# Retention with a gated MLP on one core: in the late second products, the last columns' load and scaling four steps behind the stretch, and the third stretch at step 21 in place of 20

## The chip, the cores and the metric

The kernel runs on one core of a Trainium2 chip. It is written engine by engine: PE (TensorE) multiplies matrices, and its weight loads are shown as PEld; DVE (VectorE), ACT (ScalarE) and POOL (GpSimd) work on tiles; SP (SyncE) issues nearly all of the DMAs. Each engine runs its own list of instructions in a fixed order. The metric is the device time of one execution in microseconds (us).

## What is computed

The reference, cut to what matters:

```python
scores = matmul(q, k^T) / 8                      # 8 batches, 8 heads, 576 positions, 64 wide
ret    = scores * Dmat                           # Dmat[i, j] = gamma_h ** (i - j) for i >= j, else 0
attn   = matmul(ret, v)                          # -> x: 4608 tokens x 512
h      = x @ w_in                                # 512 -> 2048
g      = h - tanh(h)
out    = g @ w_out                               # 2048 -> 512
```

## The kernel before

**Tiling.** The 576 positions of each batch are cut into 9 chunks of 64. A *column block* n is one chunk position of all 8 batches, 512 tokens. Retention goes chunk by chunk: the scores within a chunk, plus a running `state` per batch and head that carries what lies before. Each product is made in three parts, of a high and a low word of the operands (`xh`/`xl` with two words of `w_in`; `gh`/`gl` with two words of `w_out`), so a first product `mm1(n, f)` (L385) is 12 matmuls of 128x128 by 512, and a second product `mm2(n, f)` (L451) is 12 as well, three for each of the four output banks `o0` to `o3`.

**Stages.** At first the weights come in and are split into words; in that time the first products of column blocks 0 and 1 are made, and most of them are written to a spill buffer in DRAM. Then comes the *late* loop, which this case is about: 32 steps, `late = [(1, f) ...16..., (0, f) ...16...]`, each of them one second product of column block 1 (steps 0 to 15), then of block 0 (steps 16 to 31). After it, column blocks 2 to 8 run with first and second products in turn.

**A step k of the late loop** puts on the engines, in this order:
- `words(k+1)`: ACT makes the high word `gh` of the fetched column (L433), DVE the low word `gl` (L434);
- `resume(k+2)`: ACT takes the tanh `th` (L426), DVE subtracts it (L427);
- `fetch(k+4)`: SP issues the DMA of the column `s` from the spill buffer (L421). It goes into one of 3 buffers, so it waits for the `gl` of the column three before it;
- `mm2(k)`: PE makes the product. At step 15, the last one of block 1, the four banks finish one after another, and `store` copies them out: ACT `o0` and `o2` (L468), DVE `o1` and `o3` (L470); SP then issues 8 DMAs to the output (L472). Step 16 starts to fill the same four banks.

In the prediction, "the column of step 17" is the one that mm2 of step 17 uses. It is fetched at step 13, and its tanh stands on ACT in step 15, just ahead of the copies of `o0` and `o2`.

**Stretches.** Ahead of steps 3, 13 and 20 stands `entry3`, a *stretch* of retention matmuls (64x64, L257) for block 2 and the next pair's scores: batches 0 and 1 at step 3, 2 to 4 at step 13, 5 to 7 at step 20. Its end loads the data of what comes next on SP and scales it on POOL (`prep`, L207): `vr` (v and k rows, 512 KB), where it is wanted `one` (a single batch, 512 KB), and `qk` (q and k columns, 512 KB). `qk` is scaled by a table `qtab` of its column block. `qtab` has one buffer; when the pair to load is the first of a new block, `load_part` loads that block's table first (L162), and this DMA waits until POOL has made its last scaling by the old table. At step 13 the pair to load is the first of block 3, so that is where the table changes.

**Order.** `in_order` (last line of `retention_ffn`) ties every instruction to the one before it on its engine, so each engine's list, SP's too, is as the code is written. A DMA that waits on SP holds up all the DMAs behind it.

Of the kernel before, what the change touches and what calls it, by code (L numbers as in the profile page):

```python
# [59 lines left out]
def behind(tc, name):  # L60

    tc.add_manual_dep(
        tc.nc.cur_bb.bb.instructions[-1], name,
        mybir.DependencyInfo(mybir.DependencyClass.Sync, mybir.DependencyReason.DATA), reason="paced",
    )
# [3 lines left out]
def retention_ffn(ctx: ExitStack, tc: tile.TileContext, ins, out, spill):  # L69
# [86 lines left out]
    def load_qtab(c):  # L156
        if c not in qtabs:
            if c == 1:
                qtabs[c] = const.tile([P, 4, C], F32, tag="wo6", name="qtab1")
            else:  # L160
                qtabs[c] = pool.tile([P, 4, C], F32, tag="qtab", bufs=1, name=f"qtab{c}")
            nc.sync.dma_start(qtabs[c], qtab_d[c - 1])  # L162

    def load_part(j, t):

        if j >= NI:
            return
        c, b = divmod(j, B)
        if t == 0:
            load_qtab(c)  # L170
        early = c == 1 and b // 2
        if early and early > 1:

            part = const.tile([P, 2, 2, 4, C], F32, tag=f"wo{2 * (early - 2) + t}", name=f"early{j}_{t}")
        elif early and t == 1:
            part = pool.tile([P, 2, 2, 4, C], F32, tag="one", bufs=1, name=f"vr{j}")
        else:
            part = pool.tile([P, 2, 2, 4, C], F32, tag=("qk", "vr")[t], bufs=2 - t, name=f"{('qk', 'vr')[t]}{j}")
        nc.sync.dma_start(part, qkv_d[c - 1, b : b + 2, :, 2 * t : 2 * t + 2].rearrange("u p t i s -> p u t i s"))
        if early and early > 1:  # L180
            behind(tc, pace[-1])
        parts[j, t] = part
        for u in range(2):
            loaded.setdefault(j + u, Parts([None, None])).parts[t] = part[:, u]
# [12 lines left out]
    def prep(j, t, n=2):  # L197

        if j >= NI:
            return  # L200
        c = j // B
        a = parts[j, t][:, :, 0]
        if t == 0:
            table = qtabs[c].unsqueeze(1).broadcast_to([P, n, 4, C])
        else:
            table = vtab[:, c].unsqueeze(1).unsqueeze(3).broadcast_to([P, n, 4, D])
        nc.gpsimd.tensor_tensor(a, a, table, op=ALU.mult)  # L207
# [16 lines left out]
    def m_score(j, sc):  # L224
        a = loaded[j]
        return [
            (sc[half(c), i], a[half(c), 1, i, :], a[half(c), 0, i, :], True, True) for i in range(4) for c in range(2)
        ]

    def m_state(j, new):  # L230
        a = loaded[j]
        return [
            (
                new[half(c), i],
                krows[j // 4][half(c), j % 4, i, :] if j < B else a[half(c), 3, i, :],
                a[half(c), 2, i, :], True, True,
            )
            for i in range(4) for c in range(2)
        ]
# [12 lines left out]
    def run(same, other):  # L252

        while same or other:
            for ms in (same, other):
                for out_, w, x, start, stop in ms[:2]:
                    nc.tensor.matmul(out_, w, x, start=start, stop=stop)  # L257
                del ms[:2]

    def after_score(j, sc, n):  # L260

        if j < B:

            pm = pool.tile([P, 2, 4, C], F32, tag="gh", name=f"pm{j}")
            nc.vector.tensor_tensor(pm[:, 0], sc[:, 0], decay, op=ALU.mult)
        else:

            pm = parts[j, 0][:, :, 1]
            nc.vector.tensor_tensor(
                pm, sc, mask.unsqueeze(1).unsqueeze(1).broadcast_to([P, n, 4, C]), op=ALU.mult,  # L270
            )
        for u in range(n):
            scored[j + u] = pm[:, u]
# [20 lines left out]
    def bank(name, tag):  # L294
        return psp.tile([P, 2, 4, D], F32, tag=tag, bufs=2 if tag == "h" else 1, name=name)
# [5 lines left out]
    def pair(what, j, bank):  # L301
        return what(j, bank[:, 0]) + what(j + 1, bank[:, 1])
# [10 lines left out]
            more[1]()  # L313
        add_state(j, new)

    def entry3(j):


        c0, b = divmod(j, B)
        single, states = b > 0, c0 < NC - 1  # L320
        then = j + 2 + single
        o = bank(f"own{j}", "own")
        outs, scores = pair(m_out, j, o), []
        if single:
            two = bank(f"two{j + 2}", "new")
            run(m_score(j + 2, two[:, 1]), outs[:8])
            after_score(j + 2, two[:, 1:], 1)
            outs = outs[8:]
            if states:

                new = bank(f"new{j + 2}", "h")
                run(m_state(j + 2, new[:, 0]), outs[:8])
                outs = outs[8:]
                kept = pool.tile([P, 1, 4, D], F32, tag="cv", bufs=4, name=f"kept{j + 2}")
                nc.scalar.copy(kept, new[:, :1])
        if states:
            new = bank(f"new{j}", "h")
            run(pair(m_state, j, new), outs[:16])
            outs = outs[16:]
        if single:  # L340
            if not states:
                run([], outs)
            outs = m_out(j + 2, two[:, 0], True)
            if states:
                add_state(j, new)
            low = after_out(j, o, 2, False)
        if then < NI:
            sc = bank(f"s{then}", "h")
            scores = pair(m_score, then, sc)
        run(scores, outs)  # L350
        if not single:
            if states:
                add_state(j, new)
            low = after_out(j, o, 2, False)
        low()
        if then < NI:
            after_score(then, sc, 2)
        if single:
            if states:
                add_state(j + 2, kept, 1)  # L360
            after_out(j + 2, two[:, :1], 1)

        more = then % B > 0
        if then < NI:
            load_part(then, 1)
            prep(then, 1)
            if more:
                load_one(then + 2)
                prep(then + 2, 1, 1)
                prep(then + 2, 0, 1)  # L370
            load_part(then + 2 + more, 0)
            prep(then + 2 + more, 0)


    gs, ops, homes, obs = {}, {}, {}, {}
# [211 lines left out]
    first = 2 * B  # L587
    for k, (n, f) in enumerate(seq):
        last_two = k - (len(seq) - 2)
        if k in (2, 7):  # L590
            scale_k(k // 4)
        if k + 1 in early:
            scale_v(2 * early[k + 1])
        if last_two < 0:
            step()
        else:
            fetch(*late[2 + last_two])
        mm1(n, f, ("h", "o2", "h", "o3")[k % 4] if k < len(seq) - 4 else ("o2", "o3", "h", "h")[k % 4])
        if last_two < 0:
            step()  # L600
            if k < 24:
                step()
        if k in scales:
            scale_q(2 * scales[k])
        upto("load", k + (7 if k < 11 else 6))
        if k in (2, 5):
            load_pair(B + 4 + 2 * (k - 2) // 3)
        if k in (9, 10):
            load_part(first, k - 9)
        for f in [f for f in home if home[f] == (7, 13, 12, 11, 10)[k - NF]] if NF <= k < NF + 5 else []:  # L610
            nc.sync.dma_start(spill[0, f], homes[home[f]][:, (f + 1) % 2 if f > 1 else f])
        if k == 3:
            nc.sync.dma_start(krows[1], krows_d[1])
            behind(tc, pace[-1])
            sc = scores_of(3)
            ms, done = first_states(0, "new")
            run(pair(m_score, B, sc) + ms, [])
            after_score(B, sc, 2)
            done()
        if k in early:  # L620
            p = early[k]
            more = first_states(2 * (p - 3), f"o{(p + 1) % 2}") if p < B - 1 else None
            entry(2 * p, scores_of(p), more)
        if k == 14:
            load_part(first + 2, 0)
        if k == 26:
            prep(first, 1)
        if k == 28:
            prep(first + 2, 0)
    for k, (n, f) in enumerate(late):  # L630
        if k in (3, 13, 20):
            entry3(first + (0, 2, 5)[(3, 13, 20).index(k)])
        if 0 < k < len(late) - 1:
            words(*late[k + 1])
        if k < len(late) - 2:
            resume(*late[k + 2])
        if k + 4 < len(late):
            fetch(*late[k + 4])
        for _ in range(2 if k < 4 else 1):
            step()  # L640
        if k < len(late) - 1:
            mm2(n, f)
# [70 lines left out]
```

## Time and profile before

| what | value |
|---|---|
| time, median of 3 runs | 894.35 us (893.67 to 894.58) |
| time of the profiled execution | 894.74 us |
| its span, first to last instruction | 893.0 us |
| DVE busy | 368.8 us (41%) |
| ACT busy | 293.5 us (33%) |
| POOL busy | 70.3 us (8%) |
| DMA moved | 82.06 MB, mean 92 GB/s |
| late loop on PE | about 122 to 225 us of the span |

Times in the views are microseconds from the start of the span. A row of the timeline gives start, duration, engine, line, operation, output<-inputs, shapes, count, and in brackets how long the engine was idle before it and what ended that. A row of the waits gives who waited for whom, the total, the number of times and the longest. A row of the windows gives a stretch of time and the busy time of each engine in it, the TensorE clock that was granted (1.00 is full), the busy share of the DMA engines and GB/s. A row of the chain gives start, duration and what the chain ran through. Matmuls are pipelined: a 128x512 one is listed with 0.39 us while the next one starts 0.23 us later.

### The profile page before, as it was taken

The numbers are of one execution on the slowest core, as the hardware profiler recorded it, in microseconds if no ns is written. First come the engines' busy times: TensorE is split into PE (matmuls) and PEld (weight loads), VectorE is DVE, ScalarE is ACT, GpSimd is POOL, SyncE is SP. The second block draws the span as 40 slices with busy tenths as digits, with TensorE's granted clock in tenths as the row PEclk, the third lists the DMA queues.
The fourth block names the chain that finished last, engine by engine and source line by source line (L and its number), as shares of the span: only waits on it lengthen the run. The fifth ranks groups of instructions, "written<-read, shape, count | busy, mean of one in ns | idle before, by whom it ended". The sixth has DMA issues, their size and how long they took to land.

```text
span 893.0 us, 17735 instructions
## 1 busy us (share of the span) xinstructions
PE 874.8 (98%) x7848; PEld 723.6 (81%) x7848; DVE 368.8 (41%) x568; ACT 293.5 (33%) x522; POOL 70.3 (8%) x73
## 2 busy tenths in 40 slices
PE   7999999799999999999999999999999999999998
PEld 6777887588888888888888888888888888888886
DVE  6889876455333233323332334233332423223222
ACT  4787764334222222222222222222222322222222
POOL 0001002200011011101110101101110111000000
PEclk9999999999999999999999999999999999999999
DMA  9966955452212032202320131103220321002001
GB/s 346 360 201 217 345 169 166 136 160 78 60 61 77 1 95 72 79 1 64 103 69 10 49 111 44 43 6 90 72 78 1 93 73 49 1 1 47 1 1 47
DMA packets 37725, 82.06 MB, mean 92 GB/s; under 512 B 4241, under 2 KB 5393, under 8 KB 37649
## 3 DMA queue, kind: packets, MB, share of 16 engines
q1 hardware_dynamic: 37120, 80.02, 28.2%
q8 instruction: 61, 1.00, 0.5%
q10 hardware_dynamic: 528, 0.92, 0.3%
q14 instruction: 16, 0.12, 0.0%
HBM read 63.62 MB, written 17.30 MB: 91 GB/s over the span
## 4 chain that ended last, share of the span: by engine, by line
PE 85%; DMA 5%; DVE 4%; ACT 3%; issue 1%; POOL 0%; SPq 0%; DVEq 0%; POOLq 0%; ACTq 0%
PE o L451 42%; PE h L385 36%; DMA rwo<-in_w_out_dram 2%; PE new L257 2%; PE s L257 2%; PE own L257 1%; PE two L257 1%; DMA rwi<-in_w_in_dram 1%; DMA s<-spill_dram 1%; DVE mo L111 0%; DMA vr<-in_qkv_dram 0%; DVE mo L113 0%; DVE s L427 0%; DVE mo L106 0%; DMA spill_dram<-g 0%
## 5 line engine op out<-in xcount | busy, mean ns | idle before, releaser
L385 PE MATMUL h<-xh,wi 128*128 128x512 f32 x1152 | 302.4, 390 | 2.9 <-issue 1.1
L451 PE MATMUL o<-wo,gh 128*128 128x512 f32 x1144 | 292.3, 394 | 6.3 <-ACT ob L468 6.0
L451 PEld LDWEIGHTS o<-wo,gh 128*128 128x128 f32 x1144 | 213.9, 189 | 53.1 <-ACT ob L468 6.5
L385 PEld LDWEIGHTS h<-xh,wi 128*128 128x128 f32 x1152 | 215.3, 188 | 49.6 <-ACT wi L118 1.6
L412 DVE TENSOR_TENSOR g<-h,g 128x512 f32<-128x512 f32 x114 | 78.8, 691 | 341.4 <-ACT g L411 341.3
L411 ACT ACTIVATE g<-h 128x512 f32<-128x512 f32 x114 | 68.2, 598 | 364.2 <-PE h L385 362.5
L451 PE MATMUL o<-wo,gl 128*128 128x512 f32 x572 | 157.6, 390 | 0.0
L385 PE MATMUL h<-xl,wi 128*128 128x512 f32 x576 | 154.1, 389 | 0.0
L385 PEld LDWEIGHTS h<-xl,wi 128*128 128x128 f32 x576 | 108.1, 188 | 22.7
L451 PEld LDWEIGHTS o<-wo,gl 128*128 128x128 f32 x572 | 107.7, 188 | 22.6
L414 DVE TENSOR_TENSOR gl<-g,gh 128x512 fp32r<-128x512 f32 x113 | 81.4, 720 | 77.6 <-ACT gh L413 75.5
L413 ACT CAST gh<-g 128x512 fp32r<-128x512 f32 x113 | 70.1, 621 | 85.7 <-DVE g L412 85.7
L207 POOL TENSOR_TENSOR vr<-vr,vtab 128x512 f32<-128x512 f32 x21 | 23.1, 1100 | 626.9 <-DMA vr<-in_qkv_dram 540.9
L257 PE MATMUL own<-qk,state 64*64 64x64 f32 x736 | 45.2, 221 | 0.0
L257 PE MATMUL own<-qk,vr 64*64 64x64 f32 x736 | 44.1, 218 | 0.0
L257 PEld LDWEIGHTS own<-qk,vr 64*64 64x64 f32 x736 | 36.8, 135 | 0.0
L257 PEld LDWEIGHTS own<-qk,state 64*64 64x64 f32 x736 | 36.7, 134 | 0.0
L434 DVE TENSOR_TENSOR gl<-s,gh 128x512 fp32r<-128x512 f32 x30 | 22.7, 757 | 25.4 <-PE o L451 13.5
L207 POOL TENSOR_TENSOR qk<-qk,qtab 128x512 f32<-128x512 f32 x20 | 27.7, 1385 | 46.7 <-DMA qk<-in_qkv_dram 46.7
L433 ACT CAST gh<-s 128x512 fp32r<-128x512 f32 x30 | 18.6, 621 | 33.2 <-PE o L451 20.3
L427 DVE TENSOR_TENSOR s<-s,th 128x512 f32<-128x512 f32 x30 | 22.7, 757 | 8.1 <-ACT th L426 8.1
L257 PE MATMUL s<-qk 64*64 64x64 f32 x736 | 25.5, 219 | 0.0
(82 smaller groups left out, 560.6 us busy)
## 6 DMA issues: line engine op xcount, KB each, us to landing
qk<-in_qkv_dram SPq DMA_DIRECT2D x23, 512.0 KB, 5.8
vr<-in_qkv_dram SPq DMA_DIRECT2D x23, 512.0 KB, 4.4
out_dram<-ob SPq DMA_DIRECT2D x69, 128.0 KB, 2.4
rwi<-in_w_in_dram SPq DMA_DIRECT2D x16, 512.0 KB, 5.7
rwo<-in_w_out_dram SPq DMA_DIRECT2D x16, 512.0 KB, 5.3
s<-spill_dram SPq DMA_DIRECT2D x30, 256.0 KB, 2.7
one<-in_qkv_dram SPq DMA_DIRECT2D x14, 512.0 KB, 5.1
spill_dram<-g SPq DMA_DIRECT2D x20, 256.0 KB, 4.5
```

The lines of the kernel that those rows point to most:

```text
L207: nc.gpsimd.tensor_tensor(a, a, table, op=ALU.mult)
L257: nc.tensor.matmul(out_, w, x, start=start, stop=stop)
L385: nc.tensor.matmul(hp, win[f][:, a, cc, :], x[:, cc, :], start=(k == 0), stop=(k == 3 * NCC - 1))
L411: nc.scalar.activation(g, h, AF.Tanh)
L412: nc.vector.tensor_tensor(g, h, g, op=ALU.subtract)
L413: nc.scalar.copy(gh, g)
L414: nc.vector.tensor_tensor(gl, g, gh.bitcast(F32), op=ALU.subtract)
L427: nc.vector.tensor_tensor(g, g, th, op=ALU.subtract)
L433: nc.scalar.copy(gh, g)
L434: nc.vector.tensor_tensor(gl, g, gh.bitcast(F32), op=ALU.subtract)
L451: nc.tensor.matmul(ops[n][t], g[:, t * P : (t + 1) * P], wout[f_][:, a, :], start=(f_ == first and k == 0), stop=(f_ == final and k == 2),)
```

## The change

`entry3` is given a list; if it is there, the load of the last `qk` (with its table, where that is due) and its scaling are not issued at the stretch's end, but noted. The late loop issues them four steps later: for the stretch of step 3 at step 7, for that of step 13 at step 17. The third stretch stands at step 21 in place of 20, and its last load at step 25. The loads of `vr` and `one` stay at the stretches. The stretches of the later column blocks are called as before.

```diff
-    def entry3(j):
+    def entry3(j, later=None):
...
-            load_part(then + 2 + more, 0)
-            prep(then + 2 + more, 0)
+            if later is None:
+                load_part(then + 2 + more, 0)
+                prep(then + 2 + more, 0)
+            else:
+
+                later.append(then + 2 + more)
...
+    rest = []
     for k, (n, f) in enumerate(late):
-        if k in (3, 13, 20):
-            entry3(first + (0, 2, 5)[(3, 13, 20).index(k)])
+        if k in (3, 13, 21):
+            entry3(first + (0, 2, 5)[(3, 13, 21).index(k)], rest)
+        if k - 4 in (3, 13, 21):
+            load_part(rest[0], 0)
+            prep(rest.pop(), 0)
```

**SP around the second stretch.** SP's list from the stretch of step 13 to step 17, before (`s_1` is the column of step 17, `s_4` that of step 20, `ob` the output of block 1, `qtab` and `qk` the table and first pair of block 3):

```order
L193 DMA one_2087<-in_qkv_dram 128x1024
L162 DMA qtab_2091<-in_qtab_dram 128x256
L179 DMA qk_2093<-in_qkv_dram 128x2x512
L421 DMA s_1_2103<-spill_dram 128x512
L421 DMA s_2_2124<-spill_dram 128x512
L421 DMA s_3_2145<-spill_dram 128x512
L472 DMA out_dram<-ob_2150 64x512 x8
L421 DMA s_4_2179<-spill_dram 128x512
L421 DMA s_5_2204<-spill_dram 128x512
```

And the same place in the changed kernel:

```order
L193 DMA one_2087<-in_qkv_dram 128x1024
L425 DMA s_1_2098<-spill_dram 128x512
L425 DMA s_2_2119<-spill_dram 128x512
L425 DMA s_3_2140<-spill_dram 128x512
L476 DMA out_dram<-ob_2145 64x512 x8
L425 DMA s_4_2174<-spill_dram 128x512
L162 DMA qtab_2192<-in_qtab_dram 128x256
L179 DMA qk_2194<-in_qkv_dram 128x2x512
L425 DMA s_5_2204<-spill_dram 128x512
```

The table and the pair have moved past four fetches and the eight stores. In the same way the `qk` of the first stretch moves from ahead of the fetch of step 7's column to behind that of step 10's.

**DVE around the third stretch.** DVE's list there, before (`gl_5`, `s_5` belong to the column of step 21, `s_6` to that of step 22; `one<-two,mask` masks the single batch's scores within the stretch):

```order
L427 TENSOR_TENSOR s_5_2204<-s_5_2204,th_5_2243 128x512
L269 TENSOR_TENSOR one_2087<-two_2261,mask 128x256
L299 TENSOR_TENSOR state<-new_2298,state 128x512
L286 TENSOR_TENSOR xl_1748<-own_2260,xh_1747 128x2x4x64
L269 TENSOR_TENSOR qk_2093<-s_2333,mask 128x2x256
L299 TENSOR_TENSOR state<-kept_2296,state 128x256
L285 TENSOR_TENSOR xl_1748<-two_2261,xh_1747 128x4x64
L434 TENSOR_TENSOR gl_5_2378<-s_5_2204,gh_5_2377 128x512
```

And in the changed kernel:

```order
L431 TENSOR_TENSOR s_5_2204<-s_5_2204,th_5_2243 128x512
L438 TENSOR_TENSOR gl_5_2261<-s_5_2204,gh_5_2260 128x512
L431 TENSOR_TENSOR s_6_2225<-s_6_2225,th_6_2264 128x512
L269 TENSOR_TENSOR one_2087<-two_2282,mask 128x256
L299 TENSOR_TENSOR state<-new_2319,state 128x512
L286 TENSOR_TENSOR xl_1748<-own_2281,xh_1747 128x2x4x64
L269 TENSOR_TENSOR qk_2194<-s_2354,mask 128x2x256
```

The stretch's DVE work stands one step later: `gl_5` and the subtraction for `s_6` now come ahead of the mask. On ACT the stretch's copies move past `gh_5` and `th_6` in the same way, and on PE its matmuls past the 12 of step 20.

## The prediction

> **What bounds the kernel now.** The page's first row says that PE is busy for 98% of the span:
>
> ```profile
> PE 874.8 (98%) x7848; PEld 723.6 (81%) x7848; DVE 368.8 (41%) x568; ACT 293.5 (33%) x522; POOL 70.3 (8%) x73
> ```
>
> The change removes no matmul, so it can only gain what PE waits. That is the second view, the waits of PE, longest first:
>
> ```profile
> PE o L451 <- ACT ob L468: 6.0, 1, 6.0
> ...
> PE o L451 <- ACT gh L433: 0.2, 1, 0.2
> ```
>
> One wait is larger than all others together, and both rows lie in the late loop. The timeline of PE shows where:
>
> ```profile
> 171.65 0.39 PE L451 MATMUL o<-wo,gl 128*128 128x512 f32 x1
> 178.08 4.21 PE L451 MATMUL o<-wo,gh 128*128 128x512 f32 x8 [6.04 <-ACT ob L468]
> ```
>
> Step 15 ends at 171.65; step 16 wants its first bank at 171.88 (a matmul every 0.23 us) and gets it at 178.08. It waits for ACT's copy of `o0`, so ACT's timeline is next:
>
> ```profile
> 169.56 0.62 ACT L433 CAST gh<-s 128x512 fp32r<-128x512 f32 x1 [1.73 <-DVE s L427]
> 176.92 0.63 ACT L426 ACTIVATE th<-s 128x512 f32<-128x512 f32 x1 [6.75 <-DMA s<-spill_dram]
> 177.46 1.05 ACT L468 COPY ob<-o 128x512 f32<-128x512 f32 x2
> ```
>
> The two copies stand behind the tanh of step 17's column, and that waited for its DMA. Why that came late is seen on SP, first its longest wait between 160 and 186, then its timeline:
>
> ```profile
> SPq L162 <- POOL one L207: 6.1, 1, 6.1
> ```
>
> ```profile
> 163.79 0.71 SPq L193 DMA_DIRECT2D one<-in_qkv_dram  x1
> 170.66 0.33 SPq L162 DMA_DIRECT2D qtab<-in_qtab_dram  x1
> 171.04 0.43 SPq L179 DMA_DIRECT2D qk<-in_qkv_dram  x1
> 171.56 1.36 SPq L421 DMA_DIRECT2D s<-spill_dram  x3
> 178.05 6.25 SPq L472 DMA_DIRECT2D out_dram<-ob  x8
> ```
>
> POOL's rows close the chain:
>
> ```profile
> 167.35 1.57 POOL L207 TENSOR_TENSOR vr<-vr,vtab 128x512 f32<-128x512 f32 x1 [24.61 <-DMA vr<-in_qkv_dram]
> 168.88 1.06 POOL L207 TENSOR_TENSOR one<-one,vtab 128x256 f32<-128x256 f32 x1
> 169.90 0.73 POOL L207 TENSOR_TENSOR one<-one,qtab 128x256 f32<-128x256 f32 x1
> 176.38 1.27 POOL L207 TENSOR_TENSOR qk<-qk,qtab 128x512 f32<-128x512 f32 x1 [5.75 <-DMA qk<-in_qkv_dram]
> ```
>
> SP could not overwrite `qtab` before POOL's last scaling by it ended at 170.63; then 512 KB of `qk` went ahead of the fetch, which reached ACT at 176.92. So: table, SP, fetch, tanh, copy, bank, PE.
>
> The stall has a tail. The windows show the granted clock (the third last column), the chain of waits the pace:
>
> ```profile
> 172.00:175.80 3.80, 0.04 (x1) 0.00 (x0) 0.00 (x0) 0.00 (x0) 0.00 (x0) 1.00 0.93 266
> 175.90:178.00 2.10, 0.00 (x0) 0.00 (x0) 0.42 (x1) 1.08 (x3) 1.27 (x1) 0.50 0.41 156
> 178.10:182.60 4.50, 4.44 (x10) 3.16 (x11) 2.57 (x5) 1.74 (x4) 0.00 (x0) 0.50 0.51 118
> ```
>
> ```profile
> 178.93 12.70 PE o L451 x47
> ...
> 194.59 30.15 PE o L451 x132
> ```
>
> The clock halves near 175.85, 3.8 us after PE's last matmul, and is full again near 182.65. At full clock a matmul takes 30.15/132 = 0.228 us.
>
> **The change part by part.** All times are those of the profile before.
>
> *A, the stall.* 178.08 - 171.88 = **6.2 us**. How early the fetch for step 17 can now be there follows from the page's median for such a fetch and from DVE's row that frees its buffer:
>
> ```profile
> s<-spill_dram SPq DMA_DIRECT2D x30, 256.0 KB, 2.7
> ```
>
> ```profile
> 165.31 0.68 DVE L434 TENSOR_TENSOR gl<-s,gh 128x512 fp32r<-128x512 f32 x1
> ```
>
> In the changed order it stands right behind `one` and waits only for its buffer, free at 165.98. It lands between 2.7 us later, 168.7, and 5.3 later (171.56 to 176.92, behind `qk`), 171.3. I take 169.2: `one` was there by 168.88. All 6.2 us go, and what is late next is D.
>
> *B, the half clock.* The 48 matmuls from 178.08 to 178.93 + 12.70 = 191.63 take 13.5 us; at 0.228 they take 10.9. **2.5 us** go (0.1 off for the change to the stretch). They go only if no new wait of some 3.8 us comes. A short one is cheap: behind 1.08 us of idle time PE runs six matmuls in 1.55 us, full pace:
>
> ```profile
> 42.79 1.55 PE L385 MATMUL h<-xh,wi 128*128 128x512 f32 x6 [1.08 <-issue]
> ```
>
> The Trainium skill, "TensorE: Matmul & The Clock Gate", Part 1, says that the clock halves after an idle window of about 3.4 us and comes back after about 3.4 us of work. The windows agree in kind, but show 4.6 us to come back; an estimate by the page is 3.4/2 = 1.7 us for B, and the sum below would be 0.8 smaller, 887.0.
>
> *C, step 7.* The same pattern, small:
>
> ```profile
> 142.74 1.07 PE L451 MATMUL o<-wo,gl 128*128 128x512 f32 x4
> 144.06 1.20 PE L451 MATMUL o<-wo,gh 128*128 128x512 f32 x4 [0.25 <-ACT gh L433]
> ```
>
> ```profile
> 141.46 0.63 ACT L426 ACTIVATE th<-s 128x512 f32<-128x512 f32 x1 [0.88 <-DMA s<-spill_dram]
> ```
>
> Due at 142.74 + 4 x 0.228 = 143.65, come at 144.06: **0.4 us**. Its fetch came 0.88 late to ACT behind the first `qk`, which now goes behind step 10's fetch.
>
> ```profile
> 151.66 0.62 ACT L433 CAST gh<-s 128x512 fp32r<-128x512 f32 x1 [1.02 <-PE o L451]
> ```
>
> That `qk` goes out some 10 us later and is wanted at 162.5 (the row of `two` in E). It now holds up step 11's fetch by about 1 us, whose `gh` has room: it waits for PE, not for the fetch, and stands 2.7 us ahead of step 11 (144.06 + 4 x 2.73 = 155.0). Nothing.
>
> A + B + C = **9.1 us**. Against it stand three new waits.
>
> *D, the handover at step 16.* With the fetch in time, ACT does `gh` to 170.18, tanh 170.1 to 170.7, `o0` to 171.2, `o2` to 172.0 (PE ends that bank at 171.4). DVE:
>
> ```profile
> 167.94 1.53 DVE L427 TENSOR_TENSOR s<-s,th 128x512 f32<-128x512 f32 x1
> 170.21 0.98 DVE L434 TENSOR_TENSOR gl<-s,gh 128x512 fp32r<-128x512 f32 x1 [0.74 <-ACT gh L433]
> ...
> 178.19 1.28 DVE L470 COPY ob<-o 128x512 f32<-128x512 f32 x2
> ```
>
> `gl` to 171.2, the subtraction to 171.8, `o1` to 172.4, `o3` to 173.0. PE wants `o1` at 172.1 and has it at 172.45, `o3` at 172.9 and has it at 173.0: **0.45 us**. Least: 0. Most, with the fetch landing at 171.3: `o0` ready at 172.45, `o1` at 173.35, `o3` at 173.95: 0.6 + 0.65 + 0.15 = 1.4.
>
> *E, the third stretch.* Where a stretch wants its scaled pair and its mask is read from the one of step 13:
>
> ```profile
> 160.62 0.27 PE L257 MATMUL two<-one 64*64 64x64 f32 x2
> 162.55 0.23 PE L257 MATMUL two<-one 64*64 64x64 f32 x2
> ```
>
> ```profile
> 161.35 0.42 DVE L269 TENSOR_TENSOR one<-two,mask 128x256 f32<-128x256 f32 x1 [1.98 <-PE two L257]
> ```
>
> Both are wanted 1.93 us behind its start, where the scores of the next pair and the masked product (the second row of `two`) begin; the mask itself takes 0.42. Step 16 starts at 171.88, so the stretch of step 21 stands 0.45 (D) + 5 x 2.72 later, at 185.9, and wants both at 187.85.
>
> Table and `qk` now go out behind the stores. Stores from 171.6, 6.25 us as before, to 177.85; fetch for step 20 at 177.9, table 178.4, `qk` 178.8. `qk` reaches POOL 5.3 us on as before (171.04 to 176.38), at 184.1, and is scaled at 185.4: 2.4 us of margin, where at step 20 it would be 0.3 short. But the fetch for step 21 goes behind `qk` and lands near 184.7 (as 176.92 to 171.04). Tanh, subtraction, `gh` end at 186.8, step 22's tanh at 187.3, and on DVE `gl`, step 22's subtraction and only then the stretch's mask at 188.4: **0.5 us** of wait. Least 0 (stores 0.5 us quicker do it). Most 1.35: step 21's subtraction falls beside POOL's scaling of `qk`, and D's first row took 1.53 us beside POOL where A's `gl` took 0.68 without, 0.85 more.
>
> Here a rule speaks against the change, since `qk`'s scaling lay in the stall so far, where DVE had little to do. The Trainium skill, "SBUF — State Buffer", "SBUF: two separate sides", says that POOL and a DVE operation with both inputs in SBUF share ports by an exclusive lock: whoever is first holds it to its end. D's row agrees. By the rule step 21's subtraction waits up to the rest of a 1.27 us scaling, an estimate of 0.8 us more, and the sum is 887.0.
>
> *F, step 20.* Its fetch goes out at 177.9 behind the stores, lands 2.7 later at 180.6; tanh, subtraction and `gh` (0.6 to 0.7 us each with gaps between, 2.1) end at 182.7. Step 20 starts at 183.2: **0**, with 0.5 us to spare. Most, landing after 5.3: 185.3, a wait of 2.1.
>
> Moving the third stretch by one step moves its matmuls past 12 others: nothing in itself. Its `vr` and `qk` go out 5 to 10 us later and are wanted at the next stretch, which comes after the late loop: nothing.
>
> Sum: 9.1 - 0.45 - 0.5 = **8.15 us** off. The profiled execution takes 894.74 (span 893.0 and 1.74 around it): 886.6. The median of the three runs is 0.39 lower, so I forecast **886.2 us**.
>
> **The rivals.**
> *New waits in steps 16 to 21* (0.22). The load that blocked SP is not gone; it stands behind eight stores, in front of step 21's fetch. With D and F at their worst 3.5 of the 9.1 come back: 894.35 - 5.6 = **888.7**. For it: F's margin is only 0.5 us and SP's stores took 6.25 us. Against: each wait moves the later ones' due times back, so they don't add up.
> *The change doesn't free the copies* (0.05). If the fetch for step 17 is slow because the DMA engines are full (0.93 busy from 172.0 to 175.8) and not because it was issued late, ACT waits as before: **894.3**. Against: from 163.9 on only `vr` and `one` are ahead of it, and both were there by 168.9.
> *Slower* (0.03). `qk` misses the third stretch. It loses as much as was won when the scaled pair comes 6.2 us after its due time 187.85 (6.2 of waiting and 2.5 of half clock), at 194 in place of 185.4. Two more us make it **896.3**. That needs the stores to hold SP for 15 us in place of 6.25; the longest wait of SP in this stretch is 6.1.
>
> **How the numbers follow.** The forecast, with D to F between 0 and some 2 us, has 0.70: 885.2 to 887.3. The rivals have 0.22, 0.05 and 0.03. The range starts at 9.1 off less 0.3 of scatter (the three runs lie 0.9 apart), 884.9, and ends at 889.3, above the first rival. A measurement of this kernel tells 0.2%, 1.8 us, from no change: faster 0.92 (forecast and first rival), same 0.05, slower 0.03.
>
> **What would show it.** In the changed profile: no wait of PE for ACT's copies over 1 us; granted clock 1.00 from 172 to 190; the fetch for step 17 out at about 165.6 and its tanh right behind the `gh` before it; no wait at step 7; SP's 6.1 us wait for POOL gone at the second stretch; the third stretch within a microsecond of 185.5. Wrong would be: a PE wait at step 20 or in the stretch of step 21 on ACT, DVE or POOL's `qk`, or the old wait with its 6 us.

## The result and the profile after

| kernel | time, median | ratio to before, 95% interval |
|---|---|---|
| before | 894.47 us (893.67 to 895.04, 4 runs) | |
| changed | 887.30 us (887.15 to 889.93, 3 runs, and one run of 3106.18, not counted) | 0.993 [0.9906, 0.9953] |
| changed again (e1) | 886.78 us (886.58 to 887.28, 5 runs) | 0.9906 [0.9886, 0.9926] |
| changed, third time (e9) | 886.94 us (885.64 to 889.54, 6 runs) | 0.9914 [0.9898, 0.993] |

The change makes the kernel faster by 0.7 to 0.9%, and no interval holds 1. One run of the changed kernel, the one first profiled, took 3106 us with every kind of matmul slowed throughout and DVE and ACT at their usual pace; nothing is read from it, and "after" below is e1, the same kernel profiled again.

The waits of PE in the late loop of e1, to set against the 6.0 and the 0.2 us of before:

```profile
PE two L257 <- DVE one L269: 0.5, 1, 0.5
PE o L455 <- DVE ob L474: 0.2, 1, 0.2
```

The two old waits are gone and two small new ones have come, at other places. (This view counts idle time of PE alone; what each place lost in all stands in the table below.) The granted clock (third last column) stays full where it was halved:

```profile
165.00:172.00 7.00, 6.83 (x31) 5.36 (x30) 5.51 (x8) 3.95 (x8) 3.21 (x3) 1.00 0.60 175
172.00:176.00 4.00, 4.00 (x17) 3.08 (x18) 2.67 (x5) 1.62 (x3) 0.00 (x0) 1.00 0.60 178
176.00:190.00 14.00, 13.41 (x236) 11.02 (x236) 5.96 (x11) 4.59 (x9) 1.29 (x1) 1.00 0.64 181
```

SP's timeline in e1 shows why: behind `one` stands no table and no wait for POOL, but the fetches.

```profile
163.22 0.86 SPq L193 DMA_DIRECT2D one<-in_qkv_dram  x1
165.44 5.52 SPq L425 DMA_DIRECT2D s<-spill_dram  x3
171.05 6.55 SPq L476 DMA_DIRECT2D out_dram<-ob  x8
177.69 0.54 SPq L425 DMA_DIRECT2D s<-spill_dram  x1
178.31 0.40 SPq L162 DMA_DIRECT2D qtab<-in_qtab_dram  x1
178.77 0.42 SPq L179 DMA_DIRECT2D qk<-in_qkv_dram  x1
179.28 0.89 SPq L425 DMA_DIRECT2D s<-spill_dram  x2
```

The fetch for step 17 goes out at 165.44, where it went at 171.56, and ACT shows no wait for it:

```profile
169.51 0.63 ACT L430 ACTIVATE th<-s 128x512 f32<-128x512 f32 x1
170.04 0.57 ACT L472 COPY ob<-o 128x512 f32<-128x512 f32 x1
```

**A finer measure.** The runs of one kernel lie up to 5.5 us apart (before, 17 runs beside e1: 892.66 to 898.16), and in the profiles the late loop starts anywhere between 121.8 and 123.8 us, before the change can act. So I also use the **late loop**: PE's time from the first matmul of step 0 to the first first product of block 2. Before and e1, PE's timeline, first and last row of it:

```profile
122.23 1.98 PE L451 MATMUL o<-wo,gh 128*128 128x512 f32 x8
...
224.58 0.39 PE L385 MATMUL h<-xh,wi 128*128 128x512 f32 x1
```

```profile
122.32 1.98 PE L455 MATMUL o<-wo,gh 128*128 128x512 f32 x8
...
217.16 0.39 PE L389 MATMUL h<-xh,wi 128*128 128x512 f32 x1
```

That is 102.35 us before and 94.84 after, **7.5 us** less. A step's 12 matmuls take 2.72 us where nothing is late. What a step took above that (a step's own spacing from its first matmul to the next step's or stretch's first; a step ahead of a stretch is set against 2.81 us and the third stretch against 2.96, which they take where nothing is late), by PE's rows:

| place | before | e1 | forecast for e1 |
|---|---|---|---|
| steps 6 and 7 (term C) | 0.57 | 0.03 | 0 |
| wait at step 16 (A) | 6.20 | 0 | 0 |
| half clock in step 16 (B) | 2.48 | 0 | 0 |
| handover in step 16 (D) | in A | 0.64 | 0.45 |
| wait in the third stretch (E) | 0 | 1.13 | 0.5 |
| step 20 (F) | 0 | 0.05 | 0 |

### The profile page after: what moved, and what is told of

Read it like the earlier page. It is cut to its first block, busy times and chain, and to the rows that moved or that the text cites. A ratio compares the mean times of both kernels' runs of the same rounds, so it can differ in the third digit from the quotient of the medians.

```text
span 3104.4 us, 17735 instructions
## 1 busy us (share of the span) xinstructions
PE 3098.4 (100%) x7848; PEld 1715.7 (55%) x7848; DVE 367.1 (12%) x568; ACT 295.0 (10%) x522; POOL 66.9 (2%) x73
## 4 chain that ended last, share of the span: by engine, by line
PE 100%; ACT 0%; DVE 0%; issue 0%
PE o L455 46%; PE h L389 46%; PE new L257 3%; PE s L257 2%; PE own L257 1%; PE two L257 1%; PE new_first L257 0%; PE wps L502 0%; PE s_first L257 0%; PE own_first L257 0%; DVE ob L489 0%; ACT ob L488 0%; ACT xh L283 0%; DVE warm L496 0%
## 5 line engine op out<-in xcount | busy, mean ns | idle before, releaser
L389 PE MATMUL h<-xh,wi 128*128 128x512 f32 x1152 | 1014.5, 1091 | 0.5 <-ACT xh L283 0.5
L455 PE MATMUL o<-wo,gh 128*128 128x512 f32 x1144 | 985.4, 1096 | 0.0
L389 PEld LDWEIGHTS h<-xh,wi 128*128 128x128 f32 x1152 | 507.9, 441 | 436.6 <-issue 433.7
L455 PEld LDWEIGHTS o<-wo,gh 128*128 128x128 f32 x1144 | 485.8, 426 | 434.6 <-issue 427.7
L389 PE MATMUL h<-xl,wi 128*128 128x512 f32 x576 | 514.9, 1099 | 0.0
L455 PE MATMUL o<-wo,gl 128*128 128x512 f32 x572 | 514.6, 1088 | 0.0
L389 PEld LDWEIGHTS h<-xl,wi 128*128 128x128 f32 x576 | 239.0, 415 | 230.9 <-issue 230.9
L455 PEld LDWEIGHTS o<-wo,gl 128*128 128x128 f32 x572 | 231.5, 405 | 230.1 <-issue 229.8
L257 PE MATMUL own<-qk,vr 64*64 64x64 f32 x736 | 123.3, 447 | 0.0
L257 PEld LDWEIGHTS s<-qk 64*64 64x64 f32 x736 | 77.9, 367 | 5.8 <-issue 5.8
```

Of the source, the lines that this page charges most:

```text
L389: nc.tensor.matmul(hp, win[f][:, a, cc, :], x[:, cc, :], start=(k == 0), stop=(k == 3 * NCC - 1))
L455: nc.tensor.matmul(ops[n][t], g[:, t * P : (t + 1) * P], wout[f_][:, a, :], start=(f_ == first and k == 0), stop=(f_ == final and k == 2),)
```

## The experiments

Each kernel was profiled once and timed beside the kernel before, in three groups: e1 to e4, e5 to e8, and e9 to e11. Medians can be compared within a group, ratios across groups. The short diffs are against the changed kernel.

| kernel | late loop, us | time, median, us | ratio to before, 95% interval |
|---|---|---|---|
| before | 102.35 | 895.37, 893.85, 895.10 beside the three groups | |
| e2 stretch at 21 alone | 102.09 | 895.74 | 1.0005 [0.9991, 1.0019] |
| e1, e9 changed | 94.84, 94.71 | 886.78, 886.94 | 0.9906 and 0.9914, above |
| e3 late loads alone | 94.93 | 888.13 | 0.9919 [0.9901, 0.9938] |
| e4 first load at once | 95.67 | 887.42 | 0.9912 [0.9893, 0.9931] |
| e7 only the table late | 94.92 | 887.58 | 0.9932 [0.9919, 0.9944] |
| e6 copies ahead of the tanh | 93.60 | 885.96 | 0.9915 [0.9902, 0.9929] |
| e5, e10 load behind the fetch | 93.58, 93.76 | 886.26, 886.62 | 0.9913 [0.99, 0.9927], 0.9905 [0.9891, 0.9919] |
| e8 both | 93.67 | 886.1 | 0.992 [0.9907, 0.9933] |
| e11 load behind the fetch, stretch at 20 | 94.92 | 886.91 | 0.9915 [0.99, 0.9929] |

The intervals of the times tell e2 from all others, and little else; what follows on parts of a microsecond rests on the late loop of one profile each (two for the changed kernel and for e5).

**e1: the changed kernel again.**

> The changed kernel once more, since its first profile shows every matmul of the program slowed. Theory (chain of table, SP, fetch, tanh, copy, bank): A, B and C are gone, and what is left is D at step 16 (0.45 us) and E in the stretch of step 21 (0.5 us): span 884.8, time 886 to 887.5, granted clock 1.00 through 172 to 190. Rival (new waits in steps 16 to 21): a wait of 1 to 3 us at step 20 or in the stretch of step 21, time 888 to 890.

By the time, the clock (1.00) and the span (885.5 where 884.8 was expected) this is the theory's side. But the two new waits add up to 1.8 us in place of 0.95, and the larger one, 1.13 us in the stretch of step 21, is as long as the rival said (1 to 3 us). What sets them is read in the points below.

**e2: the third stretch at step 21, all loads at once.**

```diff
-            entry3(first + (0, 2, 5)[(3, 13, 21).index(k)], rest)
-        if k - 4 in (3, 13, 21):
-            load_part(rest[0], 0)
-            prep(rest.pop(), 0)
+            entry3(first + (0, 2, 5)[(3, 13, 21).index(k)])
```

> The third stretch at step 21, all loads at the stretches as before. Theory: the 6.2 us stall at step 16, the half clock and the 0.4 us at step 7 are all there, and the move itself is worth nothing: 894.0 to 894.8, as before the change. Rival (the place of the third stretch is what helps): below 892.

The waits of PE in its late loop, and a window of it:

```profile
PE o L455 <- ACT ob L472: 5.6, 1, 5.6
PE o L455 <- ACT gh L437: 0.6, 1, 0.6
```

```profile
175.10:181.80 6.70, 4.06 (x9) 2.88 (x10) 3.09 (x5) 2.64 (x5) 1.26 (x1) 0.50 0.63 184
```

Both waits and the half clock are there, with 5.6 and 0.6 us where they were 6.0 and 0.2. The median lies above the expected 894.8, as does that of the kernel before beside it, 895.37. The move alone is worth nothing; the gain belongs to the late loads.

**e3: the late loads alone**, `(3, 13, 20)` in both lines.

> The late loads with the third stretch still at step 20. Theory: A, B and C are gone as in e1; the pair for the third stretch is scaled at about 185.4 where step 20 wants it at 185.1, and its mask stands behind the subtraction for step 21, whose fetch went behind qk: 0.3 to 1.5 us of wait in the stretch in place of e1's 0.5, time 0 to 1.5 us above e1. Rival (the move to step 21 costs as much as it saves): the same as e1 within 0.3 us.

Late loop 94.93 against 94.84 and 94.71: in the stretch e3 loses as much as e1 does (1.17 and 1.13 us). PE stops at two places, and the second stop is for the mask:

```profile
184.87 0.33 PE L257 MATMUL s<-qk 64*64 64x64 f32 x4 [0.20 <-issue]
185.62 0.27 PE L257 MATMUL two<-one 64*64 64x64 f32 x2 [0.42 <-DVE one L269]
```

The first stop looks like the pair, but POOL ended the pair's scaling at 184.58, 0.3 us ahead of the row. What ended 0.1 us ahead of it is a copy on ACT, which empties the bank that the new scores take:

```profile
184.41 0.35 ACT L335 COPY kept<-new 128x256 f32<-128x256 f32 x1
```

This copy stands behind the tanh of the column whose fetch went behind `qk`, as the mask does on DVE. So in e3 as in e1 the late fetch sets the wait, with the pair only 0.1 us behind the 184.5 at which the stretch wanted it. By the late loop the rival holds: with the other edit as it is, the move to step 21 neither gains nor costs. The times don't decide it: the medians lie 1.3 us apart, which the theory allows, but e3's six runs spread over 3 us, 886.5 to 889.52, and the profiled one is the second fastest of them.

**e4: the first stretch's load at once**, `rest if k > 3 else None`.

> As the changed kernel, but the first stretch loads its qk at once, as before; only the second and third loads are late. Theory: the wait at step 7 is back, 0.4 us above e1, all else as e1. Rival (the 0.4 us are absorbed by a later wait): the same as e1.

```profile
PE o L455 <- ACT gh L437: 0.9, 1, 0.9
PE two L257 <- DVE one L269: 0.3, 1, 0.3
PE o L455 <- DVE ob L474: 0.2, 1, 0.2
```

The wait at step 7 is back, larger than before the change (0.9 against 0.2 in the view of the waits; 0.6 in e2). Steps 6 and 7 lose 1.2 us, three times what C says. ACT's tanh shows the cause, a fetch for which ACT sat idle 2.57 us; DVE's subtraction behind it took its usual 0.69 us:

```profile
143.10 0.63 ACT L430 ACTIVATE th<-s 128x512 f32<-128x512 f32 x1 [2.57 <-DMA s<-spill_dram]
```

The late loop is only 0.8 us longer than e1's, since the wait in the stretch is 0.61 in place of 1.13. That is no answer to the lateness of PE at step 7, which moves the copies and the stores just as far; what sets that wait is seen under e9.

**e7: only the table and the scaling late.**

```diff
-    def load_part(j, t):
+    def load_part(j, t, table=True):
...
-        if t == 0:
+        if t == 0 and table:
             load_qtab(c)
...
+                load_part(then + 2 + more, 0, False)
                 later.append(then + 2 + more)
...
-            load_part(rest[0], 0)
+            load_qtab(rest[0] // B)
             prep(rest.pop(), 0)
```

> As the changed kernel, but only the table and the scaling are four steps late; the 512 KB of qk go out at the stretch as before the change, ahead of the fetches. Theory (the stall was SP held by the table): SP isn't held, qk lands near 170.3 and the fetch for step 17 near 171, so step 16 waits 1.0 to 1.6 us in place of 0.64 with the clock at 1.00, the wait at step 7 is back (0.5), and the stretch of step 21 waits 0 to 0.2: late loop 94.6 to 95.6. Rival (512 KB ahead of the fetch are what hurts): step 16 waits 3 us or more, late loop above 97, with the half clock above 99.

PE's waits at step 16 and ACT's tanh ahead of the copies, e7's timeline:

```profile
171.87 0.50 PE L456 MATMUL o<-wo,gh 128*128 128x512 f32 x1 [0.46 <-ACT ob L473]
172.72 0.50 PE L456 MATMUL o<-wo,gh 128*128 128x512 f32 x1 [0.35 <-DVE ob L475]
```

```profile
170.71 0.63 ACT L431 ACTIVATE th<-s 128x512 f32<-128x512 f32 x1 [1.73 <-DMA s<-spill_dram]
```

With 512 KB of `qk` ahead of it and SP free, the fetch was there at 170.7: steps 15 and 16 lose 1.5 us (0.6 and 0.9) where e1 loses 0.64, and the granted clock stays at 1.00 from 165 to 183. So of the old stall, SP held by the table made nearly all; the 512 KB ahead make 0.9 us of it. This is also the test of the rival that the fetch was slow because the DMA engines were full: from its issue at 165.38 to the tanh at 170.71 it took 5.3 us, as long as before the change (171.56 to 176.92), so it had been late because it was issued late. In the stretch of step 21 PE loses nothing: there the fetch for step 21 stands behind the table alone.

**e5 and e10: the late load behind its step's fetch.**

```diff
-        if k - 4 in (3, 13, 21):
-            load_part(rest[0], 0)
-            prep(rest.pop(), 0)
...
         if k + 4 < len(late):
             fetch(*late[k + 4])
+        if k - 4 in (3, 13, 21):
+            load_part(rest[0], 0)
+            prep(rest.pop(), 0)
```

> As the changed kernel, but the late load stands behind its step's fetch on SP, not ahead of it: the fetch for step 21 no longer follows qk. By late loop I mean PE's time from the first matmul of step 0 to the first first product of block 2; it was 94.84 us in e1, with 1.13 us of wait in the stretch of step 21. Theory (that wait is the fetch for step 21, late behind qk, and through it the mask): the fetch lands near 182 in place of 184.9, qk is scaled 0.4 us later at about 186.1 and wanted at 187.6, the stretch waits 0 to 0.2 us, late loop 93.6 to 93.9. Rival (the wait is POOL's scaling of qk or DVE beside it): still 0.8 us or more, late loop 94.5 or more.

> e5 once more, beside e9. Theory: late loop 93.5 to 93.7, no wait in the stretch of step 21, 0.6 to 1.3 us below e9. Rival (e5's gain was another chip's scatter): within 0.3 us of e9's late loop.

DVE's timeline up to the mask, first e1, then e5:

```profile
185.61 0.69 DVE L431 TENSOR_TENSOR s<-s,th 128x512 f32<-128x512 f32 x1 [2.17 <-ACT th L430]
187.04 0.69 DVE L438 TENSOR_TENSOR gl<-s,gh 128x512 fp32r<-128x512 f32 x1 [0.74 <-ACT gh L437]
187.65 0.68 DVE L431 TENSOR_TENSOR s<-s,th 128x512 f32<-128x512 f32 x1
188.25 0.42 DVE L269 TENSOR_TENSOR one<-two,mask 128x256 f32<-128x256 f32 x1
```

```profile
184.03 1.09 DVE L438 TENSOR_TENSOR gl<-s,gh 128x512 fp32r<-128x512 f32 x1 [0.74 <-ACT gh L437]
185.04 0.68 DVE L431 TENSOR_TENSOR s<-s,th 128x512 f32<-128x512 f32 x1
185.94 0.42 DVE L269 TENSOR_TENSOR one<-two,mask 128x256 f32<-128x256 f32 x1 [0.22 <-PE two L257]
```

In e1 the mask comes behind a row of column work that started late; in e5 that work is done and the mask waits for PE. The stretch loses nothing, in both profiles; the late loop is 1.0 to 1.3 us below the changed kernel's. The chain fetch, tanh, subtraction, mask is confirmed. (One figure of the theory was off: the pair was scaled at 184.57 in e5, not at 186.1, though its load went out behind the fetch.) In the time itself e10 lies 0.3 us below e9, less than the runs scatter.

**e6: at step 15 the product and the copies ahead of the tanh.**

```diff
-        if k < len(late) - 2:
+        if k < len(late) - 2 and k != 15:
             resume(*late[k + 2])
...
             mm2(n, f)
+        if k == 15:
+            resume(*late[k + 2])
```

> As the changed kernel, but at step 15 the product and the copies of the banks stand ahead of the tanh and subtraction for step 17. Theory: the wait at step 16 (0.64 us in e1) goes, since DVE copies o1 one subtraction earlier, but the third stretch is then wanted 0.6 us earlier while its late fetch is set by SP's stores, so its wait grows from 1.13 to about 1.7: late loop 94.6 to 94.9, no gain. Rival (the two waits are independent): late loop 94.2.

Neither side: 93.60 is below both. Step 16 still takes 0.43 us too long, since bank 3 is only done when step 15 ends and its copy takes 0.7; and the stretch waits 0.20, not more than in e1. The stores went out earlier against PE: 0.74 us ahead of step 16's first matmul, 0.26 in e1, and took 6.0 us in place of 6.5. How much of that is the edit and how much the chance of a run was not tried apart.

**e8: e5 and e6 together.**

> e5 and e6 together: the late load behind its step's fetch, and at step 15 the copies ahead of the tanh. Theory: both new waits go, late loop 93.0 to 93.4, about 1.6 us below e1. Rival (the stretch then comes so early that qk, scaled at about 186, is late for it): wait of 0.5 us or more on POOL's qk at step 21, late loop 93.7 or more.

Late loop 93.67, no wait in the stretch, 0.4 us at step 16 in place of 0.6, and 0.3 us lost in steps 5 and 6, ahead of all that was edited (what costs them is read under C below). Above the expected 93.0 to 93.4 and no better than e5 or e6 alone.

**e9: the changed kernel a third time.**

> The changed kernel once more, beside e10 and e11 on one chip. Theory: late loop 94.3 to 94.9; the wait in the stretch of step 21 (1.13 us in e1, 0.61 in e4) goes with how long SP takes to issue the eight stores (6.5 us in e1, 5.9 in e4), the wait at step 16 is 0.6 again. Rival (the wait in the stretch is fixed by DVE's order): 1.1 again whatever the stores take.

Late loop 94.71, step 16 loses 0.62. The stores and the loss in the stretch, from SP's and PE's rows: e1 6.55 and 1.13 us, e9 5.81 and 0.72, e4 5.91 and 0.61. SP in e9:

```profile
171.91 5.81 SPq L476 DMA_DIRECT2D out_dram<-ob  x8
```

Longer stores go with a longer wait from e1 to the other two, but between e9 and e4 the order is turned round: the stores are not all of it. The size follows from when the fetch for step 21 arrives, that is, when its tanh starts on ACT. First e1, then e9:

```profile
184.94 0.63 ACT L430 ACTIVATE th<-s 128x512 f32<-128x512 f32 x1 [2.23 <-DMA s<-spill_dram]
185.29 0.63 ACT L430 ACTIVATE th<-s 128x512 f32<-128x512 f32 x1 [2.60 <-DMA s<-spill_dram]
```

| kernel | tanh for step 21 | stretch starts | tanh ahead by | stretch loses |
|---|---|---|---|---|
| e1 | 184.94 | 185.71 | 0.77 | 1.13 |
| e9 | 185.29 | 186.48 | 1.19 | 0.72 |
| e4 | 186.05 | 187.34 | 1.29 | 0.61 |
| e6 | 185.23 | 186.93 | 1.70 | 0.20 |

The last two columns add up to 1.90 or 1.91 us each time, and in e5, where the tanh is 3.27 us ahead, nothing is lost. So the arrival of this fetch alone gives the size of the wait; the stores act through it, and so does the fetch's own way behind `qk`.

**e11: e5 with the third stretch at step 20.**

> e5 with the third stretch back at step 20. In e5 the pair was scaled 13.8 us behind the start of step 16; at step 20 the stretch wants it 13.5 us behind. Theory: with the fetch out of the way the pair itself is the last to come, the stretch waits 0.3 to 1.2 us for POOL's qk, late loop 93.9 to 94.8; that is what the move to step 21 is worth. Rival (the place of the stretch doesn't matter, as e3 against e1): within 0.2 us of e10.

Late loop 94.92, 1.2 us above e10 (in the time 0.3 us, less than the scatter) and 0.1 above what was expected. PE and POOL in e11:

```profile
187.12 0.27 PE L257 MATMUL s<-qk 64*64 64x64 f32 x2 [0.83 <-POOL qk L207]
```

```profile
185.79 1.27 POOL L207 TENSOR_TENSOR qk<-qk,qtab 128x512 f32<-128x512 f32 x1 [14.45 <-DMA qk<-in_qkv_dram]
```

Here the stretch waits for the pair alone, and step 21 is the place where it doesn't. The size is that of one profile: the pair was scaled 14.5 us behind the start of step 16, where e5 and e10 had it 13.8 behind, which would have left some 0.3 us of wait. The move has a use, but only once the fetch is out of the way (e3 against e1: 0.1 to 0.2 us; e11 against e10: 1.2 us).

## Why the prediction was right, point by point

The forecast was 886.2 us with 884.9 to 889.3; three measurements gave 887.3 (by the ratio, 0.993 x 894.47 = 888.2), 886.8 and 886.9. The runs of one kernel lie up to 5.5 us apart, so a time this close to the forecast says little about terms of half a microsecond; they are judged by the late loop.

- **A, the stall: right in cause and size.** 6.2 forecast, 6.20 measured. e2 shows that it stays without the late loads, e7 that freeing SP of the table is enough to remove all but 0.9 us of it.
- **B, the half clock: right.** 2.5 forecast, 2.48 measured. The condition given (no new wait of some 3.8 us) held in e1, and in e7 1.5 us of waiting at step 16 left the clock at 1.00. In e2 the clock had halved by 175.1, 3.0 us after PE's last matmul, so the limit lies lower than the 3.8 us of the profile before. In both profiles the clock stayed halved for 6.83 us (175.82 to 182.65 before, 175.04 to 181.87 in e2), while PE was back at 178.08 and 177.68: the 4.6 us that the prediction read as the time to come back is 4.2 in e2. The estimate of 1.7 us worked out from the Trainium skill, "TensorE: Matmul & The Clock Gate", Part 1, was too small here.
- **C, step 7: right in size, the cause only in part.** 0.4 forecast, 0.54 measured over steps 6 and 7. The fetch behind `qk` is one cause: in e4 it alone costs 1.2 us. But in the profile of the kernel before, the late tanh of 141.46 alone would have made no wait: with a subtraction of the usual 0.69 us, `gh` would have been ready at 143.5, ahead of the 143.65 when it was due. The subtraction took 1.17 us beside POOL's scaling of the same `qk`, and the prediction doesn't have that:

```profile
142.13 1.17 DVE L427 TENSOR_TENSOR s<-s,th 128x512 f32<-128x512 f32 x1 [0.54 <-ACT th L426]
141.01 1.74 POOL L207 TENSOR_TENSOR qk<-qk,qtab 128x512 f32<-128x512 f32 x1
```

The change moves load and scaling together, so the term came out in e1 though its cause was told only in part. In e7 the fetch was in time, the scaling still came early (140.25), and steps 6 and 7 lost 0.4 us. Nor is the place clean once the load is late: POOL's scaling of `vr` and `one` stays there, and in e9, the same kernel as e1, steps 5 and 6 lost 0.38 us beside it (0.3 in e8):

```profile
138.46 1.40 DVE L438 TENSOR_TENSOR gl<-s,gh 128x512 fp32r<-128x512 f32 x1
139.78 1.10 DVE L431 TENSOR_TENSOR s<-s,th 128x512 f32<-128x512 f32 x1
```

From step 3 to step 7, set against e6, which lost least, the profiles with an early load lost 0.45 to 1.3 us (before, e2, e4, e7), those with a late one 0 to 0.44 (the eight others).

- **D, the handover: right mechanism, too small.** 0.45 forecast, 0.64 measured (0.62 in e9). DVE's two copies set it, as said; PE loses a little more around them than the two due times gave.
- **E, the third stretch: right mechanism, too small by half.** 0.5 forecast, 1.13 and 0.72 measured. e5 and e10 confirm that the fetch for step 21 behind `qk` sets it, and the table under e9 that its arrival gives the size. In e1 it arrived 13.6 us behind the start of step 16, where the sum had 12.8: the stores took 6.55 in place of 6.25, the issues after them and the way behind `qk` some 0.25 each more than charged. A piece was left out: the scores also want ACT's copy `kept`, which stands behind step 22's tanh. PE stopped 0.27 us for it in e1, but within the time that it would have waited for the mask anyway. The prediction called a wait of PE in this stretch a sign of being wrong; it is one, in a term that was named and forecast at half its size.
- **The rule on the shared ports (the Trainium skill, "SBUF — State Buffer").** Step 21's subtraction took 0.69 us in e1, as without POOL: it came when the scaling was all but done (185.61, and POOL ended at 185.70). In e5 a `gl` did meet the scaling and took 1.09. So the cost is real and was missed here by the order of events, not excluded; in steps 5 to 7 it did cost PE time, as C shows.
- **F: right, but with nothing to spare.** In e1 the `gh` of step 20 ended 0.13 us ahead of its use (182.71 and 182.84) where 0.5 was forecast, and step 20 took 0.05 us too long; in e9 nothing was lost.
- **The sum.** 8.15 forecast; the late loop shortened by 7.5. The difference is D and E, 0.8 us together, less C's 0.15. The mean times, each set against the kernel before beside it, fell by 6.3, 8.4 and 7.7 us.
- **The rivals.** New waits in steps 16 to 21 are there, but with 1.8 us, not 3.5. "Doesn't free the copies" fell with e1, where ACT copied `o0` at 170.04, and with e7. The slower one never came near: the pair was scaled at 185.7 in e1, 2 us ahead of its use.

One statement of the prediction was only half true: at step 20 the stretch would lack 0.3 us for its pair. In e3 the pair was 0.1 us late, but what PE waited for there was `kept` and the mask, which are late at either step, so the move to 21 saved nothing in this change; the pair itself is waited for in e11 alone.

## What to carry to other kernels

When PE waits on a cheap copy, follow the copying engine's list back to the first instruction that waited, and from there the queue that issued its DMA: here a 128 KB table with one buffer held a queue for 6 us, and with it a fetch that nobody had connected with the table. Moving such a load behind a burst of stores frees one fetch and delays the next one, so move it behind the fetch of its step as well (e5: 1.0 to 1.3 us of the late loop, though too little to show in the time), and ask whether what it feeds must then come a step later (e11). And where a fetch and a scaling on POOL stand at the same place, look at both before one is called the cause (C).

## What the runs showed of the hardware that was not expected

- **One store in eight is slow to issue.** Of the eight stores of 128 KB at step 15, seven take SP 0.54 to 0.6 us each, and one, the fifth, sixth or seventh, 0.9 to 2.1 us, in all twelve profiles (1.77 before, 2.07 in e1, 1.39 in e9, 0.89 in e2). What holds it was not found. It makes E's size in part a matter of the run.
- **A DVE operation beside POOL ends a fixed time after POOL's.** The subtraction of 1.53 us before the change ended 0.55 us after POOL's scaling of `vr` did (169.47 and 168.92), e5's `gl` of 1.09 us 0.55 after POOL's scaling of `qk` (185.12 and 184.57). The same holds for all 75 subtractions and `gl` of the late columns that took over 0.85 us in the twelve profiles: each ended 0.55 us after an operation of POOL; undisturbed they take 0.68. That fits what the Trainium skill, "SBUF — State Buffer", "SBUF: two separate sides", describes as an exclusive lock.
